# RWKV-6 attention and a maxout layer on one core: loads issued three units ahead, the decay DMAs on another queue, the maxout written with relu, and the weights prepared beside unit 0

## The chip, the core and the metric

The kernel runs on one core of a Trainium2 chip. The time is device time in microseconds for one execution. Five engines work side by side: TensorE (PE, whose weight loads are shown as PEld), VectorE (DVE), ScalarE (ACT), GpSimd (POOL) and SyncE (SP). SP computes nothing here, it only issues DMAs. Each engine takes its instructions in program order, DMA issues among them.

## What is computed

```python
# r, k, v, w: (batch 4, heads 8, seq 768, head_dim 48); u: (heads, head_dim)
for t in range(S):
    cur = outer(u * k[t], v[t])                 # per batch and head, 48 x 48
    y[t] = r[t] @ (state + cur)
    state = w[t][:, None] * state + outer(k[t], v[t])
x = y.transpose(0, 2, 1, 3).reshape(4 * 768, 384)   # tokens x (heads * head_dim)
h1, h2 = x @ w1, x @ w2                         # 384 x 1024 each
out = maximum(h1, h2) @ w_out                   # 1024 x 384 -> (3072, 384)
```

## The kernel before

The sequence is cut into 6 chunks of 128 tokens, and the 4 batches into 2 pairs. A **unit** n is one chunk c = n // 2 of one pair of batches: 12 units. Inside a unit 64 partitions belong to each batch, and each partition holds two consecutive tokens (`i`). The recurrence is done chunk by chunk: logarithms of w (`logw`, ACT, then `lp` on GpSimd), cumulated by a matmul with a triangular matrix (`cumsum`), turned back by exponentials (`exps`), multiplied onto r and k (`scale_rk`, DVE), transposed on TensorE (`transp`, with a DVE copy), multiplied to scores (`scores`), and so on to y (`y_inter`, `y_intra`), which is transposed to x (`xt`, ending in the ACT copy of line 367). The bonus with u is made on GpSimd (`bonus_mul`, `bonus_sum`). For odd chunks but the last, the decay of the whole chunk pair is needed with the head dimension on partitions: `exps` writes one row per batch to DRAM (`row`, line 236) and `decay_load` reads it back transposed (`WL`, line 243, 1024 elements of 4 bytes); both DMAs are issued from the ACT queue, four times each in all (units 2, 3, 6 and 7). `decay_exp` and `decay` use WL one step later.

The maxout is written as max(h1, h2) = |h1 - h2| / 2 + (h1 + h2) / 2. So `gate` multiplies x by wd = w1 - w2 and takes the absolute value (ACT, line 381), and `outp` adds two products: x by wc = (w1 + w2) (w_out / 2), which is folded once, and the gated part by w_out / 2. wd, w1 + w2, its transposes and wc are made by `weights_gate` and `weights_out`.

`step(a, t, g, o)` writes out by hand the order in which four units at different stages are worked on: unit a is being loaded and scaled, unit t transposed and multiplied, units g and o gated and given out. The main loop runs step(n, n - 1, n - 2, n - 2) for n from 3 to 13. **Step n** means that call. Ahead of it stand the first units, one stage after the other: `step(a=0)`, `step(t=0)`, `weights_gate`, `step(a=1, g=0)`, `weights_out`, `step(t=1, o=0)`, `step(a=2)`.

Loads and stores are all issued by SP, in program order. `load(n)` is eight DMAs of 192 KB (w, k, r, v, for each of two batches; runs of 384 bytes). It stands at the start of step n - 2. The buffers for k, r and v are four deep, those for w three deep. `outp` ends in a store of 192 KB from `osb` (four buffers); the store's destination is `out[tok:tok + C, :].rearrange("(q i) n -> i q n", i=2)`, so its outermost dimension has size 2. Each step from the first gated unit on has two stores, behind that step's load in SP's order.

Of the kernel before, what the change touches and what calls it, by code (L numbers as in the profile page):

```python
# [8 lines left out]
F32 = mybir.dt.float32  # L9
BF16 = mybir.dt.bfloat16  # L10
AF = mybir.ActivationFunctionType
# [23 lines left out]
def _body(tc, r, k, v, w, u, moe_w1, moe_w2, moe_w_out, out):  # L35
    nc = tc.nc
    B, H, S, D = r.shape
    P = 128
# [8 lines left out]
    DP = 64  # L47
# [21 lines left out]
    def odd(n):  # L69
        return unit(n)[0] % 2 == 1  # L70

    def last(n):
        return unit(n)[0] == NC - 1
# [5 lines left out]
    def load(n):  # L79
        c, b0 = unit(n)  # L80
        d = {}
        for name, src in (("w", w), ("k", k), ("r", r), ("v", v)):
            t = ldp.tile([P, H, 2, D], F32, tag="l" + name, name="l" + name,
                         bufs=3 if name == "w" else 4)
            for b in range(2):
                nc.sync.dma_start(  # L86
                    out=t[b * Q:(b + 1) * Q].rearrange("p h i d -> p h (i d)"),
                    in_=src[b0 + b, :, c * C:(c + 1) * C, :].rearrange(
                        "h (p i) d -> p h (i d)", i=2))
            d[name] = t  # L90
        L[n] = d
# [4 lines left out]
    w1f = const.tile([P, KO, d_ff], F32)  # L96
    w2f = const.tile([P, KO, d_ff], F32)
    wof = const.tile([P, FO, HD], F32)
    nc.sync.dma_start(out=w1f, in_=moe_w1.rearrange("(o p) n -> p o n", p=P))
    nc.sync.dma_start(out=w2f, in_=moe_w2.rearrange("(o p) n -> p o n", p=P))  # L100
    load(1)
    nc.sync.dma_start(out=wof, in_=moe_w_out.rearrange("(o p) n -> p o n", p=P))
    load(2)
    load(3)


    triS = const.tile([P, P], F32)
    make_upper_triangular(nc, triS, val=1.0, diag=False)
    triI = const.tile([P, P], F32)
    make_upper_triangular(nc, triI, val=1.0, diag=True)  # L110
    tri2 = const.tile([P, P], F32)
    nc.gpsimd.memset(tri2, 0.0)
    ones2 = const.tile([P, P], F32)
    nc.gpsimd.memset(ones2, 0.0)
    for b in range(2):
        nc.gpsimd.memset(ones2[b * Q:(b + 1) * Q, b * Q:(b + 1) * Q], 1.0)
    ident = const.tile([P, P], BF16)
    make_identity(nc, ident)
    mask = const.tile([P, 2, 2, Q], F32)
    sel = const.tile([P, 2, 2, Q], BF16)  # L120
    nc.gpsimd.memset(sel, 0.0)
    for b in range(2):
        q = slice(b * Q, (b + 1) * Q)
        nc.gpsimd.tensor_copy(tri2[q, q], triS[q, q])
        for i in range(2):
            nc.gpsimd.tensor_copy(sel[q, i, i, :], ident[q, q])
            for i2 in range(2):
                nc.gpsimd.tensor_copy(mask[q, i, i2, :],
                                      (triI if (i, i2) == (0, 1) else triS)[q, q])

    NRK = 2
    rkn_b = []
    for i in range(NRK):
        t = const.tile([P, 2, 2, H, DP], BF16, name=f"rkn{i}")
        nc.vector.memset(t, 0.0)
        rkn_b.append(t)
    MZ = [const.tile([P, 2, H, DP], F32, name=f"mz{i}") for i in range(2)]
    for t in MZ:
        nc.gpsimd.memset(t, 0.0)

    S_f = [const.tile([P, 2, NP, D], F32, name=f"Sf{g}") for g in range(2)]
    T_f = [const.tile([P, 2, NP, D], F32, name=f"Tf{g}") for g in range(2)]
# [2 lines left out]
        nc.vector.memset(S_f[g], 0.0)  # L145
        nc.vector.memset(S_b[g], 0.0)
    WL = [const.tile([P, 2, NP], F32, name=f"WL{i}") for i in range(2)]
    for t in WL:
        nc.vector.memset(t, 0.0)

    wd_sb = const.tile([P, KO, d_ff], BF16)
    ws_sb = const.tile([P, KO, d_ff], BF16)
    wo_sb = const.tile([P, FO, HD], BF16)
    wsT_sb = const.tile([P, FO, HD], BF16)
    wc_sb = const.tile([P, KO, HD], BF16)

    def weights_gate():
        for ko in range(KO):
            nc.vector.tensor_sub(wd_sb[:, ko, :], w1f[:, ko, :], w2f[:, ko, :])

    def weights_out():
        for ko in range(KO):
            nc.vector.tensor_add(ws_sb[:, ko, :], w1f[:, ko, :], w2f[:, ko, :])  # L163
        nc.scalar.mul(wo_sb, wof, 0.5)
        for ko in range(KO):
            tp = pt_([P, FO, P], BF16, "tr")
            for fo in range(FO):
                nc.tensor.transpose(tp[:, fo, :], ws_sb[:, ko, fo * P:(fo + 1) * P], ident)
            nc.vector.tensor_copy(
                wsT_sb.rearrange("p f (k c) -> p k f c", k=KO)[:, ko, :, :], tp)  # L170
        for ko in range(KO):
            wc_p = pt_([P, HD], F32, "go", 2)
            for fo in range(FO):
                nc.tensor.matmul(wc_p, wsT_sb[:, fo, ko * P:(ko + 1) * P],  # L174
                                 wo_sb[:, fo, :], start=(fo == 0), stop=(fo == FO - 1))
            nc.vector.tensor_copy(wc_sb[:, ko, :], wc_p)

# [6 lines left out]
    def logw(n):  # L184
        s = U[n] = {}
        s["lw"] = lw = wt_([P, H, 2, D], F32, "lw")
        nc.scalar.activation(lw, L[n]["w"], AF.Ln)  # L187
        s["lp"] = lp = wt_([P, H, D], F32, "lp", 4)
        nc.gpsimd.tensor_add(lp, lw[:, :, 0, :], lw[:, :, 1, :])  # L189

    def bonus_mul(n):
        s = U[n]
        s["vb"] = vb = wt_([P, H, 2, D], BF16, "vb", 3)
        nc.gpsimd.tensor_copy(vb, L[n]["v"])
        s["rku"] = rku = wt_([P, H, 2, D], F32, "rku", 1)
        nc.gpsimd.tensor_mul(rku, L[n]["r"], L[n]["k"])  # L196
        nc.gpsimd.tensor_mul(  # L197
            byi(rku), byi(rku),
            u_b.rearrange("p (h d) -> p h d", h=H).unsqueeze(1).to_broadcast([P, 2, H, D]))
# [27 lines left out]
    def exps(n):  # L227
        s = U[n]
        mz = s["mz"]
        nc.scalar.activation(s["A"][:, 1], mz[:, 0, :, 0:D], AF.Exp)  # L230
        s["iA"] = iA = wt_([P, 2, H, D], F32, "iA", 1)
        nc.scalar.activation(iA, mz[:, :, :, 0:D], AF.Exp, scale=-1.0)
        if last(n) or not odd(n):
            return
        s["row"] = row = drp.tile([2, H * DP], F32, tag="row", name="row")
        nc.scalar.dma_start(out=row, in_=mz[Q - 1::Q, 1].rearrange("b h d -> b (h d)"))

    def decay_load(n):
        if last(n) or not odd(n):
            return  # L240
        s = U[n]
        s["WL"] = wl = WL[n % 2]
        nc.scalar.dma_start(out=wl.rearrange("d b p -> d (b p)"),
                            in_=s["row"].rearrange("b (p x) -> x (b p)", x=P))

    def scale_rk(n):
# [53 lines left out]
    def carry(n):  # L300
        if not odd(n):
            state_cast(unit(n)[1] // 2)
# [66 lines left out]
    def gate(n, j):  # L369
        s = U[n]  # L370
        if j == 0:
            s["gT"] = wt_([P, FO, 2, P], BF16, "gT")
        g = pt_([P, 2, 2 * P], F32, "go", 2)
        for f in range(2):
            fo = 2 * j + f
            for ko in range(KO):
                nc.tensor.matmul(g[:, f, :], wd_sb[:, ko, fo * P:(fo + 1) * P],  # L377
                                 s["xT"][:, ko].rearrange("p j t -> p (j t)"),
                                 start=(f == 0 and ko == 0), stop=(f == 1 and ko == KO - 1),
                                 skip_group_check=True)  # L380
        nc.scalar.activation(s["gT"][:, 2 * j:2 * j + 2].rearrange("p f j t -> p f (j t)"), g,  # L381
                             AF.Abs)

    def outp(n, b):
        c, b0 = unit(n)
# [12 lines left out]
        nc.sync.dma_start(out=dst, in_=osb)  # L398


    def step(a=None, t=None, g=None, o=None, ahead=True):

        A, T, G, O = a is not None, t is not None, g is not None, o is not None
        if T: decay_load(t)
        if T: transp(t, 0)
        if A: cumsum(a)
        if G: gate(g, 0)
        if T: transp(t, 1)
        if A: exps(a)
        if A: bonus_mul(a)  # L410
        if G: gate(g, 1)
        if T: kv(t)
        if T: scores(t, 0)
        if A and ahead and a + 1 < NU: logw(a + 1)
        if T and t >= 1: decay_exp(t - 1)
        if T and t >= 1: decay(t - 1)
        if G: gate(g, 2)
        if G: gate(g, 3)
        if T: scores(t, 1)
        if T: y_inter(t)  # L420
        if T: carry(t)
        if A: scale_rk(a)
        if A: bonus_sum(a)
        if O: outp(o, 0)
        if T: y_intra(t)
        if O: outp(o, 1)
        if T: xt(t)

    logw(0)
    step(a=0, ahead=False)  # L430
    step(t=0)
    weights_gate()
    logw(1)
    step(a=1, g=0, ahead=False)
    weights_out()
    step(t=1, o=0)
    logw(2)
    load(4)
    step(a=2)
    for n in range(3, NU + 2):  # L440
        if n + 2 < NU:
            load(n + 2)
        step(n if n < NU else None, n - 1 if n - 1 < NU else None, n - 2, n - 2)

    ps.release()
# [34 lines left out]
```

## Time and profile before

| | us |
|---|---|
| median of 3 runs | 228.42 (227.33 to 229.29) |
| the profiled execution | 227.37 |
| its span, first to last instruction | 225.4 |

The profile is of one execution. Besides the page it answers queries: what each engine and SP's queue waited for, the busy time and the share of the 16 DMA engines in any stretch, the instructions in order of time, and the chain of work that ended last. Durations below are of that execution, counted from the start of its span.

### The profile page before, as it was taken

What the parts mean: (1) busy time and instruction counts of PE and PEld (TensorE: products, weight loads), DVE (VectorE), ACT (ScalarE), POOL (GpSimd) and SP (SyncE); (2) the same over time, 40 slices, a digit from 0 to 9 for tenths busy, and PEclk for the clock granted to TensorE, in tenths of its full rate; (3) what the DMA queues carried; (4) which work ended last, traced back from release to release, by engine and by line L of the source; (5) the groups of instructions that cost most, each with busy time, mean ns of one, the idle gap of its engine ahead of it and who ended that gap; (6) DMA issues with size and microseconds to landing.
All of it is one profiled execution on the core that took longest, in us unless ns stands there. A gap on an engine that the chain in (4) does not pass through costs nothing.

```text
span 225.4 us, 5068 instructions
## 1 busy us (share of the span) xinstructions
PE 157.4 (70%) x2116; PEld 103.7 (46%) x2116; DVE 117.2 (52%) x138; ACT 89.9 (40%) x150; POOL 108.3 (48%) x115
## 2 busy tenths in 40 slices
PE   0214472486936999885997859869979699988910
PEld 0013351353513757563574635645746466665600
DVE  5097829546029766858165490580683845660000
ACT  2120437000352754563445533634554546354500
POOL 8584094001076934994957805638469493200000
PEclk9999999596695999999999997997999999999995
DMA  6999998920003389648356448555564831111110
GB/s 127 227 412 260 243 273 188 193 70 3 9 31 59 84 172 182 130 131 181 87 143 149 107 109 153 141 130 126 143 154 118 188 74 50 52 53 43 47 43 37
DMA packets 59990, 28.86 MB, mean 128 GB/s; under 512 B 54968, under 2 KB 59192, under 8 KB 59968
## 3 DMA queue, kind: packets, MB, share of 16 engines
q1 hardware_dynamic: 55792, 28.51, 54.3%
q10 hardware_dynamic: 4176, 0.03, 1.1%
q8 instruction: 16, 0.26, 0.5%
q14 instruction: 6, 0.05, 0.1%
HBM read 23.81 MB, written 4.73 MB: 127 GB/s over the span
## 4 chain that ended last, share of the span: by engine, by line
PE 27%; DMA 27%; SPq 20%; DVE 7%; ACT 6%; POOL 4%; issue 4%; ACTq 0%; POOLq 0%; DVEq 0%
SPq L86 17%; DMA lw<-in_w_dram 12%; PE go L392 9%; DMA lk<-in_k_dram 6%; PE go L389 4%; DMA row<-mz 4%; PE go L377 3%; DMA WL<-row 3%; PE go L174 2%; DVE ws_sb L163 2%; ACT gT L381 2%; DMA lr<-in_r_dram 2%; ACT xT L367 2%; SPq L398 2%; PE ex L218 2%
## 5 line engine op out<-in xcount | busy, mean ns | idle before, releaser
L377 PE MATMUL go<-xT,wd_sb 128*128 128x256 bf16 x288 | 38.0, 277 | 2.3 <-ACT xT L367 1.5
L392 PE MATMUL go<-wo_sb,gT 128*128 128x384 bf16 x192 | 38.1, 345 | 0.0
L189 POOL TENSOR_TENSOR lp<-lw 128x384 f32<-128x384 f32 x12 | 14.6, 1216 | 44.9 <-ACT lw L187 44.7
L321 DVE TENSOR_TENSOR M<-sc,mask 128x1024 bf16<-128x1024 f32 x24 | 29.4, 1223 | 8.2 <-PE sc L318 8.2
L395 ACT COPY osb<-go 128x384 f32<-128x384 f32 x24 | 11.5, 479 | 54.8 <-PE go L392 54.8
L377 PEld LDWEIGHTS <-wd_sb 128*128 128x128 bf16 x288 | 27.5, 100 | 11.2 <-issue 6.3
L381 ACT ACTIVATE gT<-go 128x512 bf16<-128x512 f32 x48 | 27.4, 589 | 7.1 <-PE go L377 6.9
L389 PE MATMUL go<-wc_sb,xT 128*128 128x384 bf16 x72 | 17.4, 354 | 13.2 <-ACT gT L381 13.1
L206 POOL TENSOR_TENSOR vd<-lv,dg 128x768 bf16<-128x768 f32 x12 | 18.6, 1550 | 16.5 <-DVE dg L204 16.0
L392 PEld LDWEIGHTS <-gT 128*128 128x128 bf16 x192 | 19.8, 103 | 14.7 <-issue 3.4
L262 DVE COPY rT<-tr 128x1024 bf16<-128x1024 bf16 x12 | 8.3, 688 | 32.2 <-PE tr L257 32.2
L224 DVE TENSOR_TENSOR mz<-ex,lw 128x384 f32<-128x384 f32 x12 | 6.7, 558 | 34.9 <-ACT A L223 34.9
L257 PE MATMUL tr<-ident,rkn 128*128 128x128 bf16 x192 | 15.9, 230 | 12.0 <-DVE rkn L249 8.3
L218 PE MATMUL ex<-lp,tri 128*128 128x384 f32 x24 | 12.5, 606 | 15.0 <-POOL lp L189 12.7
L197 POOL TENSOR_TENSOR rku<-rku,u_b 128x768 f32<-128x768 f32 x12 | 22.4, 1864 | 0.9
L196 POOL TENSOR_TENSOR rku<-lr,lk 128x768 f32<-128x768 f32 x12 | 21.7, 1810 | 0.0
L257 PEld LDWEIGHTS <-rkn 128*128 128x128 bf16 x192 | 13.1, 103 | 14.4 <-DVE rkn L249 10.1
L187 ACT ACTIVATE lw<-lw 128x768 f32<-128x768 f32 x12 | 10.1, 845 | 23.7 <-DMA lw<-in_w_dram 23.4
L307 POOL CAST Sb<-Sf 64x384 bf16<-64x384 f32 x20 | 10.8, 538 | 15.9 <-DVE Sf L290 15.0
L250 DVE TENSOR_TENSOR rkn<-lk,iA 128x768 bf16<-128x768 f32 x12 | 16.2, 1352 | 0.0
L249 DVE TENSOR_TENSOR rkn<-lr,A 128x768 bf16<-128x768 f32 x12 | 15.2, 1271 | 1.0 <-ACT A L230 0.8
L223 ACT ACTIVATE A<-ex 128x384 f32<-128x384 f32 x12 | 5.9, 491 | 24.7 <-PE ex L218 24.7
(61 smaller groups left out, 209.8 us busy)
## 6 DMA issues: line engine op xcount, KB each, us to landing
lw<-in_w_dram SPq DMA_DIRECT2D x24, 192.0 KB
lk<-in_k_dram SPq DMA_DIRECT2D x24, 192.0 KB
lr<-in_r_dram SPq DMA_DIRECT2D x24, 192.0 KB
lv<-in_v_dram SPq DMA_DIRECT2D x24, 192.0 KB
out_dram<-osb SPq DMA_DIRECT2D x24, 192.0 KB
w1f<-in_moe_w_dram SPq DMA_DIRECT2D x1, 1536.0 KB
w2f<-in_moe_w_dram SPq DMA_DIRECT2D x1, 1536.0 KB
wof<-in_moe_w_out_dram SPq DMA_DIRECT2D x1, 1536.0 KB
```

The costliest lines, as they stand in the source:

```text
L86: nc.sync.dma_start(out=t[b * Q:(b + 1) * Q].rearrange("p h i d -> p h (i d)"), in_=src[b0 + b, :, c * C:(c + 1) * C, :].rearrange("h (p i ...
L196: nc.gpsimd.tensor_mul(rku, L[n]["r"], L[n]["k"])
L197: nc.gpsimd.tensor_mul(byi(rku), byi(rku), u_b.rearrange("p (h d) -> p h d", h=H).unsqueeze(1).to_broadcast([P, 2, H, D]))
L206: nc.gpsimd.tensor_mul(byi_inv(vd), L[n]["v"], dg.to_broadcast([P, H, 2, D]))
L218: nc.tensor.matmul(ex, tri2, lp.rearrange("p h d -> p (h d)"), start=not odd(n), stop=True)
L250: nc.vector.tensor_mul(rkn[:, 1, :, :, 0:D], byi(L[n]["k"]), s["iA"])
L257: nc.tensor.transpose(tp[:, p, :, i, :], s["rkn"][:, x, i, 2 * p:2 * p + 2, :].rearrange("s r d -> s (r d)"), ident)
L321: nc.vector.tensor_mul(M.rearrange("s e p t -> s (e p) t"), sc.rearrange("s e p t -> s (e p) t"), mask[:, i].rearrange("s i q -> s (i q)") ...
L377: nc.tensor.matmul(g[:, f, :], wd_sb[:, ko, fo * P:(fo + 1) * P], s["xT"][:, ko].rearrange("p j t -> p (j t)"), start=(f == 0 and ko == 0) ...
L381: nc.scalar.activation(s["gT"][:, 2 * j:2 * j + 2].rearrange("p f j t -> p f (j t)"), g, AF.Abs)
L389: nc.tensor.matmul(o, s["xT"][:, ko, b, :], wc_sb[:, ko, :], start=(ko == 0), stop=False)
L392: nc.tensor.matmul(o, s["gT"][:, fo, b, :], wo_sb[:, fo, :], start=False, stop=(fo == FO - 1))
```

## The change

- `load(n + 3)` stands at the start of step n, `load(4)` ahead of `step(a=1, g=0)` and `load(5)` ahead of the next; w2 is loaded first, then w1 and w_out, then `load(1)` to `load(3)`.
- The DMAs `row` and `WL` are issued from GpSimd's queue. `row` has its own function, called behind `bonus_mul`.
- max(h1, h2) = relu(h1 - h2) + h2: `gate` ends in Relu, wc = w2 w_out, and w_out is no longer halved. The three additions w1 + w2 are gone; w2 is cast on ACT and w_out on GpSimd.
- The transposes of w2 (`weights_turn`, copies now on ACT), `weights_gate` and `weights_out` stand between the parts of unit 0, ahead of step(a=1, g=0). Units 2 and 1 share one step, step(a=2, t=1, o=0).
- Some constants are made after `logw(0)`; the zeroing of MZ moves from GpSimd to DVE, that of WL is dropped.

```diff
+    nc.sync.dma_start(out=w2f, in_=moe_w2.rearrange("(o p) n -> p o n", p=P))
     nc.sync.dma_start(out=w1f, in_=moe_w1.rearrange("(o p) n -> p o n", p=P))
-    nc.sync.dma_start(out=w2f, in_=moe_w2.rearrange("(o p) n -> p o n", p=P))
+    nc.sync.dma_start(out=wof, in_=moe_w_out.rearrange("(o p) n -> p o n", p=P))
     load(1)
-    nc.sync.dma_start(out=wof, in_=moe_w_out.rearrange("(o p) n -> p o n", p=P))
     load(2)
     load(3)
...
+    def weights_cast():
+        for ko in range(KO):
+            nc.scalar.copy(w2_sb[:, ko, :], w2f[:, ko, :])
+        for h in range(2):
+            f = slice(h * FO // 2, (h + 1) * FO // 2)
+            nc.gpsimd.tensor_copy(wo_sb[:, f], wof[:, f])
...
-    def weights_out():
-        for ko in range(KO):
-            nc.vector.tensor_add(ws_sb[:, ko, :], w1f[:, ko, :], w2f[:, ko, :])
-        nc.scalar.mul(wo_sb, wof, 0.5)
+    def weights_turn():
         for ko in range(KO):
             tp = pt_([P, FO, P], BF16, "tr")
             for fo in range(FO):
-                nc.tensor.transpose(tp[:, fo, :], ws_sb[:, ko, fo * P:(fo + 1) * P], ident)
-            nc.vector.tensor_copy(
-                wsT_sb.rearrange("p f (k c) -> p k f c", k=KO)[:, ko, :, :], tp)
+                nc.tensor.transpose(tp[:, fo, :], w2_sb[:, ko, fo * P:(fo + 1) * P], ident)
+            nc.scalar.copy(w2T_sb.rearrange("p f (k c) -> p k f c", k=KO)[:, ko, :, :], tp)
+
+    def weights_out():
         for ko in range(KO):
             wc_p = pt_([P, HD], F32, "go", 2)
             for fo in range(FO):
-                nc.tensor.matmul(wc_p, wsT_sb[:, fo, ko * P:(ko + 1) * P],
+                nc.tensor.matmul(wc_p, w2T_sb[:, fo, ko * P:(ko + 1) * P],
                                  wo_sb[:, fo, :], start=(fo == 0), stop=(fo == FO - 1))
...
+    def decay_row(n):
         if last(n) or not odd(n):
             return
+        s = U[n]
         s["row"] = row = drp.tile([2, H * DP], F32, tag="row", name="row")
-        nc.scalar.dma_start(out=row, in_=mz[Q - 1::Q, 1].rearrange("b h d -> b (h d)"))
+        nc.gpsimd.dma_start(out=row, in_=s["mz"][Q - 1::Q, 1].rearrange("b h d -> b (h d)"))
...
-        nc.scalar.dma_start(out=wl.rearrange("d b p -> d (b p)"),
+        nc.gpsimd.dma_start(out=wl.rearrange("d b p -> d (b p)"),
                             in_=s["row"].rearrange("b (p x) -> x (b p)", x=P))
...
         nc.scalar.activation(s["gT"][:, 2 * j:2 * j + 2].rearrange("p f j t -> p f (j t)"), g,
-                             AF.Abs)
+                             AF.Relu)
...
         if A: bonus_mul(a)
+        if A: decay_row(a)
         if G: gate(g, 1)
         if T: kv(t)
         if T: scores(t, 0)
-        if A and ahead and a + 1 < NU: logw(a + 1)
+        if A and a + 1 < NU and a > 0: logw(a + 1)
...
     logw(0)
-    step(a=0, ahead=False)
-    step(t=0)
+    constants()
+    step(a=0)
+    weights_cast()
+    transp(0, 0)
+    transp(0, 1)
+    kv(0)
+    scores(0, 0)
+    scores(0, 1)
+    y_inter(0)
+    weights_turn()
+    y_intra(0)
     weights_gate()
+    carry(0)
+    xt(0)
+    weights_out()
     logw(1)
-    step(a=1, g=0, ahead=False)
-    weights_out()
-    step(t=1, o=0)
-    logw(2)
     load(4)
-    step(a=2)
+    step(a=1, g=0)
+    load(5)
+    step(a=2, t=1, o=0)
     for n in range(3, NU + 2):
-        if n + 2 < NU:
-            load(n + 2)
+        if n + 3 < NU:
+            load(n + 3)
         step(n if n < NU else None, n - 1 if n - 1 < NU else None, n - 2, n - 2)
```

## Rows read from the trace of the kernel before

**Rows 1.** The page: span; DMA share and GB/s in 40 equal slices; the chain's shares.

```profile
span 225.4 us, 5068 instructions
...
DMA  6999998920003389648356448555564831111110
GB/s 127 227 412 260 243 273 188 193 70 3 9 31 59 84 172 182 130 131 181 87 143 149 107 109 153 141 130 126 143 154 118 188 74 50 52 53 43 47 43 37
...
PE 27%; DMA 27%; SPq 20%; DVE 7%; ACT 6%; POOL 4%; issue 4%; ACTq 0%; POOLq 0%; DVEq 0%
```

**Rows 2.** What engines waited for, whole span: total us, times, longest.

```profile
ACT lw L187 <- DMA lw<-in_w_dram: 23.4, 9, 3.8
...
PE go L389 <- ACT gT L381: 13.1, 7, 2.9
```

**Rows 3.** The DMA view of 187 to 206 us: packets, then queues (share of 16 engines).

```profile
DMA packets 623, 0.98 MB, mean 52 GB/s; under 512 B 8, under 2 KB 620, under 8 KB 620
...
q1 hardware_dynamic: 620, 0.94, 13.2%
```

**Rows 4.** Stretches: us, busy by engine (instructions), PE clock, DMA share, GB/s.

```profile
48.00:60.00 12.00, 9.46 (x138) 5.25 (x136) 5.22 (x7) 1.10 (x2) 1.00 (x2) 0.72 0.01 1
60.00:94.70 34.70, 26.69 (x365) 17.35 (x363) 22.82 (x25) 17.55 (x31) 22.24 (x16) 0.90 0.57 106
94.70:183.20 88.50, 72.47 (x1079) 48.43 (x1078) 49.18 (x61) 42.74 (x76) 55.75 (x51) 0.96 0.57 135
183.20:224.30 41.10, 29.26 (x350) 19.86 (x348) 11.19 (x13) 15.77 (x27) 6.27 (x5) 0.95 0.13 48
224.30:225.40 1.10, 0.00 (x0) 0.00 (x0) 0.00 (x0) 0.00 (x0) 0.00 (x0) 0.50 0.00 0
```

**Rows 5.** The DMA view of 94.7 to 183.2 us, SP's queue.

```profile
q1 hardware_dynamic: 26902, 11.80, 55.1%
```

**Rows 6.** SP's queue in order of time: start, us, line, out<-in, number of DMAs.

```profile
59.13 10.32 SPq L398 DMA_DIRECT2D out_dram<-osb  x2
...
179.12 37.12 SPq L398 DMA_DIRECT2D out_dram<-osb  x10
```

**Rows 7.** What SP's queue waited for on the decay DMAs, whole span.

```profile
SPq L398 <- DMA row<-mz: 9.1, 1, 9.1
SPq L86 <- DMA WL<-row: 8.8, 4, 3.5
...
SPq L86 <- DMA row<-mz: 8.0, 2, 5.8
```

**Rows 8.** The DMA view of 20 to 26 us, when only loads were moving.

```profile
DMA packets 3213, 1.23 MB, mean 204 GB/s; under 512 B 3200, under 2 KB 3212, under 8 KB 3212
```

**Rows 9.** The chain that ended last, 35 to 72 us: start, us, what.

```profile
36.16 4.68 DVE ws_sb L163 x3
...
44.30 4.88 PE go L174 x24
...
62.69 0.75 ACT lw L187
...
69.86 1.04 PE tr L257 x8
```

**Rows 10.** ACT in order of time: the last instruction of steps 10 to 12.

```profile
184.57 0.80 ACT L367 COPY xT<-ex 128x768 bf16<-128x768 bf16 x1
...
196.88 0.80 ACT L367 COPY xT<-ex 128x768 bf16<-128x768 bf16 x1
...
207.49 0.80 ACT L367 COPY xT<-ex 128x768 bf16<-128x768 bf16 x1
```

**Rows 11.** Lines 243 and 50: number, duration ns min/median/max, first and last start.

```profile
L243 ACTq DMA_DIRECT2D WL<-row x4: 361/377/398, 68.9 to 141.6; - x4
...
L50 ACT ACT_TABLE_LOAD  x1: 1283/1283/1283, 0.7 to 0.7; - x1
```

**Rows 12.** The page: the ACT queue's DMA packets.

```profile
q10 hardware_dynamic: 4176, 0.03, 1.1%
```

More of the change, by code (lines that the diff above doesn't have):

```diff
@@ L108, in _body @@
     make_upper_triangular(nc, triS, val=1.0, diag=False)
-    triI = const.tile([P, P], F32)
-    make_upper_triangular(nc, triI, val=1.0, diag=True)
     tri2 = const.tile([P, P], F32)
     nc.gpsimd.memset(tri2, 0.0)
[L113 to L121, printed above, removed]
     for b in range(2):
@@ L124, in _body, with constants @@
         nc.gpsimd.tensor_copy(tri2[q, q], triS[q, q])
[L125 to L129, printed above, removed]
-    NRK = 2
[L132 to L136, printed above, removed]
+    ident = const.tile([P, P], BF16)
+    make_identity(nc, ident)
+    triI = const.tile([P, P], F32)
+    ones2 = const.tile([P, P], F32)
+    mask = const.tile([P, 2, 2, Q], F32)
+    sel = const.tile([P, 2, 2, Q], BF16)
+    def constants():
+        make_upper_triangular(nc, triI, val=1.0, diag=True)
+        nc.gpsimd.memset(sel, 0.0)
+        for b in range(2):
+            q = slice(b * Q, (b + 1) * Q)
+            for i in range(2):
+                nc.gpsimd.tensor_copy(sel[q, i, i, :], ident[q, q])
+                for i2 in range(2):
+                    nc.gpsimd.tensor_copy(mask[q, i, i2, :],
+                                          (triI if (i, i2) == (0, 1) else triS)[q, q])
+        nc.gpsimd.memset(ones2, 0.0)
+        for b in range(2):
+            q = slice(b * Q, (b + 1) * Q)
+            nc.gpsimd.memset(ones2[q, q], 1.0)
+    NRK = 2
     MZ = [const.tile([P, 2, H, DP], F32, name=f"mz{i}") for i in range(2)]
-    for t in MZ:
-        nc.gpsimd.memset(t, 0.0)
+    rkn_b = [const.tile([P, 2, 2, H, DP], BF16, name=f"rkn{i}") for i in range(NRK)]
+    for i in range(2):
+        nc.vector.memset(MZ[i], 0.0)
+        nc.vector.memset(rkn_b[i], 0.0)
     S_f = [const.tile([P, 2, NP, D], F32, name=f"Sf{g}") for g in range(2)]
@@ L147, in _body @@
     WL = [const.tile([P, 2, NP], F32, name=f"WL{i}") for i in range(2)]
-    for t in WL:
-        nc.vector.memset(t, 0.0)
     wd_sb = const.tile([P, KO, d_ff], BF16)
-    ws_sb = const.tile([P, KO, d_ff], BF16)
+    w2_sb = const.tile([P, KO, d_ff], BF16)
     wo_sb = const.tile([P, FO, HD], BF16)
-    wsT_sb = const.tile([P, FO, HD], BF16)
+    w2T_sb = const.tile([P, FO, HD], BF16)
     wc_sb = const.tile([P, KO, HD], BF16)
+    def weights_cast():
[4 more added lines that the diff above has]
+            nc.gpsimd.tensor_copy(wo_sb[:, f], wof[:, f])
     def weights_gate():
@@ L398, in outp, with step @@
         nc.sync.dma_start(out=dst, in_=osb)
-    def step(a=None, t=None, g=None, o=None, ahead=True):
+    def step(a=None, t=None, g=None, o=None):
         A, T, G, O = a is not None, t is not None, g is not None, o is not None
```

## The prediction, made before the changed kernel was run

> **What bounds the kernel now.** Four views, in this order. First the page: no engine is busy all the time, and the chain that ended last spends 47% of itself on DMAs and on SP's queue [rows 1]. So the question is which transfer is late, and why. Second, the waits: ACT waited nine times for w to land, 23.4 us in all, and of that 13.1 us in seven waits came through to TensorE, which stood with gT missing [rows 2]. That looks like a load that is asked for too late, and the change asks for it a step earlier. Third, the DMA view of a stretch in which only stores move: 187 to 206 us. There 620 packets, 0.94 MB, took 13.2% of 16 engines for the whole 19 us, which is 2.1 engines, without a pause [rows 3]. So a store of 196.6 KB runs on two of the 16 engines alone (its outermost dimension has size 2), at 0.94 MB / 19 us = 49.5 GB/s: 3.97 us each, and two stores follow each other rather than sharing. Fourth, the table of stretches [rows 4]. From 94.7 to 183.2 us the queue moved 11.80 MB [rows 5], which is six loads (8 x 196.6 KB = 1.573 MB each) and twelve stores: 88.5 / 6 = 14.75 us for a load and two stores. TensorE alone does not need that: a step with no load to wait for took 12.31 us, and the one after it, which has no new unit, 10.61 [rows 10]. The two engines that carry the stores carry their sixteenth of every load too, and queues are worked off in order, so a load that stands behind two stores lands some 8 us later on these two than on the rest. I read the late w as that, not as a late issue.
>
> If so, the kernel is paced by **this pair of DMA engines**, and a ledger of the pair's time must add up to the span. Loads alone move at 204 GB/s [rows 8], 1.573 MB / 204 = 7.7 us a unit. Up to 48 us: the first four units and the weights, busy throughout. 48 to 60: idle, share 0.01 [rows 4]. 60 to 94.7: two stores and two loads, 7.9 + 15.4 = 23.3 us of 34.7, so 11.4 idle. Then 88.5 busy. From 183.2 to 224.3 ten stores, 39.7 us of 41.1 [rows 4, 6]. That is all 24 stores and 12 loads, and the pair idles 12 + 11.4 + 1.4 = 24.8 us. Why it idles: up to 60 us SP has nothing to issue, since load(4) stands behind the first stores in program order and the first store waits for the first result (issued at 59.13 [rows 6]); after that SP stops for the landing of `row` and `WL`, which ACT issues: 9.1 + 8.8 + 8.0 us in seven waits [rows 7].
>
> **The change part by part.** *Loads three units ahead.* load(4) and load(5) now stand ahead of the first store. Their buffers (units 0 and 1, and w of units 1 and 2) come free as these units are scaled, before about 45 us by the order of before, so the pair goes on from 48 us: 2 x 7.7 = 15.4, to 63.4. The first stores are then due; before, the first was issued at 59.13 [rows 6] with the whole weight work still ahead of it, so they are ready. Worth the 12 us of idle time and, with the next item, the 11.4.
>
> *Decay DMAs on GpSimd's queue.* ACT's issue of `WL` is 0.38 us [rows 11], four times, beside other work: nothing. What counts is whether SP still stops for them. Stops of 16.8 us on loads [rows 7] fell mostly on a pair that still had DMAs queued; I take 0.25 us off each of six cycles, 14.5 us instead of 14.75. Bounds: 14.75 (nothing) and 14.0 (4.5 us in all). The Trainium skill (DMA: Bandwidth & Descriptors, Issuing engines are not separate DMA queues) speaks against a gain here: issuing from several engines only saves the sequencer's issue time. By the row, SP waited 25.9 us for DMAs of another queue; by the page the cycle would stay at 14.75 and the sum below 1.5 us longer.
>
> What it costs GpSimd is not in the trace. Bounds: 0.4 us for an issue as on ACT [rows 11], and 10 us if 1024 elements are written out one by one at what a packet of that queue took (1.1% of 16 x 225.4 us over 4176 packets is 9.5 ns [rows 12]). I take the near row, about 1 us. Cover: GpSimd was busy 55.75 of 88.5 us [rows 4], 9.1 us of a cycle of 14.5, and the `WL` issue is queued ahead of `bonus_mul`, `lp` of the next unit, `decay` and `vd`; those have the 5.4 us left over. WL is used one step later.
>
> *Relu, folding, weights beside unit 0.* The additions (4.68 us) and the folding stood on the chain from 36.16 to 49.2 us [rows 9]; gone or earlier now. The separate step(a=2), 62.69 to 69.86 [rows 9], joins the step before it. Together up to 20 us off TensorE's path. But on the pair they are worth only what lets the stores be ready at 63.4, and that they are even if nothing were gained. I cost them at nothing; the pair's queue hides them. Casts on ACT and GpSimd instead of DVE fall in the first 30 us, when the engines wait for weights to land; the weights being 4.7 MB at about 410 GB/s [rows 1], their new order moves load(1) some 4 us back, and w of unit 1 is not needed before unit 0 is through. Relu for Abs: the same pass.
>
> *What is late next.* TensorE needs about 12.3 us a step against 14.5 of the pair, so it gains on the pair until `osb` (four buffers) is full: `outp` of a step then waits for the stores of two steps before. That wait replaces the one for w, and costs nothing while the pair is busy. At the end the last load has landed and the pair needs only 7.94 us a step; steps 11 to 13 need 12.3, 10.6 and about 8 [rows 10]. Laid out, the last two stores are ready 1 to 2 us before the pair gets to them.
>
> **The sum.** 48.0 (as before) + 15.4 (load(4), load(5)) + 6 x 14.5 = 87.0 (six loads, twelve stores) + 12 x 3.97 = 47.6 (the last twelve stores) = 198.0. From the last packet to the end 1.1 [rows 4]: span 199.1. Around the span lie 227.37 - 225.4 = 2.0 us: **201 us**. The profiled execution lies 1.1 us under the median of the runs shown, 0.5%, which I leave in the range. Against before that is the 24.8 us of idle time and the 1.5 of stops.
>
> **The rivals.** *The pair is not the limit, TensorE is.* For it: the 20 us of the prologue and the 13.1 us of waits [rows 2] both lie on TensorE's path. Against it: the ledger adds up. Step 2 would end near 56 us, then nine steps of 12.3, 10.6 and 8.2, two stores 8.8 and 3.1 around: about 197.
>
> *SP still stops for the decay DMAs.* If DMAs of GpSimd share with SP's whatever made it wait, the stops stay, and those around steps 2 and 3 may again cost part of the 11.4 us. Against it: TensorE is ahead of the pair now, so `row` and `WL` are through before SP comes to them. Between 1.5 and 11.4 us: about 208.
>
> *GpSimd becomes the bound; this is the one that ends on the other side.* Place: `WL` issued in steps 3, 4, 7 and 8, with everything of the unit queued behind it. Spare per cycle is 5.4 us, steps 3 to 8 have six of them, and about 8 us of lead come from the prologue: some 40 us in all. At the upper price of 10 us four issues just fit. To lose the whole gain of 26 us they would have to take (40 + 26) / 4 = 16 us each; only then is it slower, at 229 and up. Between 10 and 16 us it lands at 203 to 225. The Trainium skill (DMA: Bandwidth & Descriptors, SWDGE vs HWDGE vs iDMA) says that descriptors of DMAs issued from GpSimd are computed by a program on its cores, which no row here shows.
>
> *Relu needs another table than Exp and Ln.* One load was 1.28 us, once [rows 11]; six switches a step would be 8 us over eleven steps, and TensorE waits for gT: slower, 270 or more. For it nothing but that Relu does not occur before; Abs needed no second load.
>
> **How the numbers follow.** Forecast (196 to 206) 0.61; TensorE paces it (about 197) 0.11; stops remain (208) 0.12; GpSimd 203 to 225, 0.08; GpSimd slower 0.03; Relu 0.02; something that leaves the time within 1% of before 0.03. What a measurement here can tell from no change is about 1%. The likeliest gives 201. The range takes in the lower bound of the cycle (3 us off: 198), TensorE's own pace with some of its margin (195), and the two cases that end at 208 and a little over: 195 to 212. Faster 0.92, within 1% 0.03, slower 0.05.
>
> **What would show it.** Right: no stretch of DMA share near zero before 190 us; ACT no longer waits for w, but before `osb` for stores; a load and two stores every 14 to 14.8 us; the last twelve stores back to back, at two engines' share; SP without waits for `row` and `WL`. Wrong: idle stretches of the pair left in the middle; or cycles well under 14 us, which would mean that the pair is not in order or not the bound; or a GpSimd busy all through steps 3 to 8; or more than one table load.

## The result, and the profile after

The changed kernel took 201.3 us (median of four runs, 200.4 to 201.9) against 228.9 of the kernel before in the same session: a ratio of 0.880, interval 0.875 to 0.886. The forecast was 201. The profiled execution has a span of 199.6 us (forecast 199.1) and lies 2.25 us below the time of that run. So the number was right. The experiments below show that the reasons given for it were right about what the bound is, and wrong about which part of the change lifted the idle time. (In e10 one execution of four and in e12 two were longer at a lower granted TensorE clock; the ratios leave these out, the medians don't, so there the ratio counts, and that of e12 rests on two executions.)

The page of after: span, DMA share and GB/s in 40 slices, the queue of the decay DMAs, shares of the chain.

```profile
span 199.6 us, 5075 instructions
...
DMA  5999999999998573483593593583581111111110
GB/s 118 210 380 400 291 203 203 203 203 198 201 175 145 143 167 100 128 185 86 144 201 80 151 164 92 146 174 92 151 166 53 50 50 54 50 53 47 48 42 32
...
q0 software_dynamic: 256, 0.03, 0.4%
...
PE 23%; DMA 17%; ACT 5%; DVE 1%; issue 1%; SPq 0%; ACTq 0%; DVEq 0%
```

Against [rows 1]: the hole near 50 us is gone, no slice before the last one is empty, and SP's queue has left the chain (it held 20%). The decay DMAs, 4176 packets of ACT's queue before [rows 12], are 256 of a software queue.

What engines waited for in after, whole span (total us, times, longest):

```profile
ACT osb L404 <- DMA out_dram<-osb: 13.2, 5, 3.7
...
ACT lw L193 <- DMA lw<-in_w_dram: 3.2, 1, 3.2
```

The nine waits for w [rows 2] have become one, of the first unit; five waits of `osb` for stores stand in their place, as forecast. Among SP's waits there is none left for `row` or `WL` [rows 7]. There is one table load, as before.

The table of stretches of after (us, busy by engine, clock, DMA share, GB/s), and the DMA view of its long stretch, 64.5 to 150.1 us:

```profile
48.00:59.50 11.50, 10.90 (x143) 6.76 (x140) 7.49 (x9) 4.62 (x8) 10.70 (x10) 0.85 1.12 189
59.50:64.50 5.00, 5.00 (x93) 3.27 (x91) 4.46 (x6) 2.59 (x6) 2.22 (x3) 1.00 0.92 145
64.50:150.10 85.60, 77.29 (x1199) 53.25 (x1189) 53.40 (x68) 47.33 (x86) 67.08 (x57) 0.98 0.59 139
150.10:198.50 48.40, 34.21 (x431) 22.85 (x428) 15.79 (x18) 18.08 (x32) 9.91 (x8) 0.94 0.14 49
198.50:199.60 1.10, 0.00 (x0) 0.00 (x0) 0.00 (x0) 0.00 (x0) 0.00 (x0) 0.50 0.00 0
```

```profile
q1 hardware_dynamic: 26837, 11.73, 57.5%
```

These are the forecast's own stretches. Each DMA counts its landing up on a semaphore, and the trace holds the times of these updates, though its views don't print them. By them the last part of load(5) landed at 64.55 us (63.4 forecast); then 11.73 MB, six loads and twelve stores, take 85.6 us, 14.27 a cycle (14.5); the last twelve stores take 48.4 (47.6) at two engines' share (0.14); 1.1 us follow. The errors are +1.1, -1.4 and +0.8: 0.5 us in all.

### The profile page after: what moved, and what is told of

The parts are those of the page before. It is cut to its first block, busy times and chain, and to the rows that moved or that the text cites. A ratio compares the mean times of both kernels' runs of the same rounds, so it can differ in the third digit from the quotient of the medians.

```text
span 199.6 us, 5075 instructions
## 1 busy us (share of the span) xinstructions
PE 151.4 (76%) x2116; PEld 101.8 (51%) x2116; DVE 108.9 (55%) x132; ACT 91.9 (46%) x155; POOL 120.3 (60%) x123
## 5 line engine op out<-in xcount | busy, mean ns | idle before, releaser
L401 PE MATMUL go<-wo_sb,gT 128*128 128x384 bf16 x192 | 36.3, 334 | 0.0
L404 ACT COPY osb<-go 128x384 f32<-128x384 f32 x24 | 11.5, 479 | 49.6 <-PE go L401 34.6
L212 POOL TENSOR_TENSOR vd<-lv,dg 128x768 bf16<-128x768 f32 x12 | 17.7, 1475 | 21.5 <-DVE dg L210 21.3
L195 POOL TENSOR_TENSOR lp<-lw 128x384 f32<-128x384 f32 x12 | 12.0, 1001 | 18.5 <-ACT lw L193 18.5
L202 POOL TENSOR_TENSOR rku<-lr,lk 128x768 f32<-128x768 f32 x12 | 22.5, 1871 | 0.0
L224 PE MATMUL ex<-lp,tri 128*128 128x384 f32 x24 | 11.6, 569 | 12.2 <-POOL lp L195 7.2
L316 POOL CAST Sb<-Sf 64x384 bf16<-64x384 f32 x20 | 18.1, 904 | 2.0 <-PE y L349 1.1
L398 PE MATMUL go<-wc_sb,xT 128*128 128x384 bf16 x72 | 15.8, 329 | 0.0
L327 PE MATMUL sc<-rT,kT 48*64 48x128 bf16 x384 | 10.5, 229 | 5.9 <-DVE M L330 2.9
L259 DVE TENSOR_TENSOR rkn<-lk,iA 128x768 bf16<-128x768 f32 x12 | 14.2, 1182 | 0.0
L210 DVE TENSOR_REDUCE dg<-rku 128x16 f32<-128x768 f32 x12 | 11.3, 944 | 3.6 <-POOL rku L203 3.6
```

The source lines that it names most:

```text
L212: nc.gpsimd.tensor_mul(byi_inv(vd), L[n]["v"], dg.to_broadcast([P, H, 2, D]))
L224: nc.tensor.matmul(ex, tri2, lp.rearrange("p h d -> p (h d)"), start=not odd(n), stop=True)
L316: nc.gpsimd.tensor_copy(S_b[g][q, :, :, e * D:(e + 1) * D], S_f[g][q])
L398: nc.tensor.matmul(o, s["xT"][:, ko, b, :], wc_sb[:, ko, :], start=(ko == 0), stop=False)
L401: nc.tensor.matmul(o, s["gT"][:, fo, b, :], wo_sb[:, fo, :], start=False, stop=(fo == FO - 1))
L404: nc.scalar.copy(osb, o)
```

## The experiments

Twelve more kernels were run. Ratios are to the kernel before, run beside each (its median was 228.0 to 229.0).

```
                                                       us      ratio  (interval)
e1  after, stores on 16 engines                       187.3   0.817  (0.811 to 0.823)
e2  before, stores on 16 engines                      208.6   0.910  (0.904 to 0.915)
e3  after, loads two ahead                            200.6   0.875  (0.870 to 0.881)
e4  before, loads three ahead                         234.3   1.024  (1.016 to 1.031)
e5  after, decay DMAs on ACT                          218.8   0.958  (0.951 to 0.966)
e6  before, decay DMAs on GpSimd                      216.6   0.951  (0.944 to 0.957)
e7  before, decay DMAs on GpSimd, loads three ahead   211.9   0.928  (0.921 to 0.935)
e8  after, decay DMAs on ACT, loads two ahead         214.2   0.939  (0.932 to 0.946)
e9  after, stores halved by columns, two engines      209.5   0.917  (0.914 to 0.921)
e10 e7 with logw(2) moved up                          208.5   0.914  (0.911 to 0.917)
e11 e1 with loads two ahead                           187.8   0.823  (0.820 to 0.826)
e12 e10 with steps 1 and 2 merged                     203.4   0.885  (0.880 to 0.891)
```

**Is the pair of engines that carries the stores the bound?** e1 and e2 take the stores off the pair and leave the rest:

```diff
-        nc.sync.dma_start(out=dst, in_=osb)
+        for i in range(2):
+            nc.sync.dma_start(out=dst[i], in_=osb[i * Q:(i + 1) * Q])
```

> The changed kernel; each store is issued as two DMAs of 64 partitions, whose outermost dimension is 64 instead of 2. Theory (the two DMA engines that carry the stores pace the kernel): the pair falls away as the limit, the DMA share is no longer 0.14 when only stores move, TensorE paces the steps at about 12 us each from 54.7 us on: 54.7 + ten steps of 10.6 to 12.3 (119) + 8.2 + 2.5 = 184 us span, about 186 us. Rival (loads asked for in time are what helped, the stores are a side matter): no change, 200 to 202 us.

Measured: 187.3 us. The page of e1, span and its rows PE and DMA, then what `osb` waited for:

```profile
span 185.1 us, 5103 instructions
...
PE   0320657974989989999899898998989988989790
...
DMA  5999999999999999999899595993011030120303
```

```profile
ACT osb L404 <- PE go L401: 43.7, 24, 5.1
```

Now all 24 copies to `osb` wait for TensorE's matmuls, and no wait for a store is left. At the end the DMA engines stand idle between stores, and PE is busy for nine tenths or near it from 50 us on: TensorE is the bound. Without the pair the rest of the kernel needs 187 us, so 14 of the 201 are the pair's. The number of engines shows in the semaphore updates too: a store has 3 in before and in after, one of them well ahead of the other two (60.6 against 66.8 us for the first store in after), and so has each half in e9 below; each half of a store in e1 and e2 has 16, as a load has.

> The kernel before, with this one edit: each store as two DMAs of 64 partitions. Loads stay two units ahead, decay DMAs on ACT's queue, old order of the first units. Theory: step 3 starts near 70 us as before, then steps of about 12 us without waits for w: 70 + 12.5 + 108 + 8.2 + 2.5 = 201 us span, 203 us. Rival (w is late because it is asked for too late): the waits for w stay, 225 to 229 us.

Measured: 208.6, 20 us under before. The page of e2, DMA share:

```profile
DMA  5999999980000228996996284974999943020203
```

The hole from 46 to 67 us stays, as it does not come from the pair; what is behind it runs without the pair's pace. The time expected was 5 to 6 us too low, but far from the rival. SP still stands 35.2 us for `row` and `WL` in e2; whether these are the missing 5 to 6 us stays open.

e9 is the control: it issues as many DMAs as e1, but on the same two engines.

```diff
-        nc.sync.dma_start(out=dst, in_=osb)
+        for f in range(2):
+            nc.sync.dma_start(out=dst[:, :, f * HD // 2:(f + 1) * HD // 2],
+                              in_=osb[:, f * HD // 2:(f + 1) * HD // 2])
```

> The changed kernel with each store issued as two DMAs of 192 columns; each keeps the outermost dimension of size 2. This is the control for the store cut into two DMAs of 64 partitions, which took 187.3 us. Theory (two engines carry the stores and pace the kernel; the number of DMAs is not what helped): the share of the DMA engines in the last store-only stretch stays near 0.14, and the time is 200 to 206 us, since packets half as long do not go faster on the two engines. Rival (more stores in flight is what gained, not more engines): 186 to 192 us.

Measured: 209.5, slower than the theory allowed. The DMA view of e9, 165 to 200 us, when only stores move:

```profile
DMA packets 2108, 1.63 MB, mean 47 GB/s; under 512 B 32, under 2 KB 2105, under 8 KB 2105
...
q1 hardware_dynamic: 2105, 1.59, 13.6%
```

Still two engines' share, at 47 GB/s with packets of 768 bytes instead of 49 to 50 with 1536. That is 5 us over 24 stores; the other 3 of the 8 us are not explained. So more DMAs are not what helped e1. Whether the shorter packets or the doubled number of DMAs lowered the rate, e9 does not tell.

**What was the lead of the loads worth?** e3 takes it out of the changed kernel, e4 puts it alone into the kernel before. The edit of e4 (that of e3 is its reverse, with load(5) left to the loop):

```diff
     logw(1)
+    load(4)
     step(a=1, g=0, ahead=False)
+    load(5)
     weights_out()
     step(t=1, o=0)
     logw(2)
-    load(4)
     step(a=2)
...
-        if n + 2 < NU:
-            load(n + 2)
+        if n + 3 < NU:
+            load(n + 3)
```

> The changed kernel with loads two units ahead as before (load(4) ahead of step 2, load(n + 2) in step n). Theory: the pair's work is the same and it still has no idle stretch, only the order changes, so 200 to 204 us; ACT waits for w again, as in the kernel before, and it costs nothing. Rival (the lead of the loads is what helped): 210 us or more.

> The kernel before with loads three units ahead, nothing else changed. Theory: the pair goes on at 48 us with load(4) and load(5) and is through with them when the first stores are ready; the stops for the decay DMAs stay: 203 to 209 us. Rival (the prologue and the decay queue carry the gain): 220 us or more.

Measured: 200.6 without the lead (after has 201.3, and the intervals overlap). The theory of e3 held, with the waits for w that it expected:

```profile
ACT lw L193 <- DMA lw<-in_w_dram: 12.7, 5, 3.3
```

They cost nothing. But e3 takes away less than its name says. Since units 2 and 1 share a step, load(4), ahead of that step, still stands ahead of the first stores; only load(5) and the later ones move behind stores. SP's queue in e3:

```profile
42.79 1.74 SPq L86 DMA_DIRECT2D lw<-in_w_dram  x2
...
52.14 3.22 SPq L407 DMA_DIRECT2D out_dram<-osb  x2
55.41 2.74 SPq L86 DMA_DIRECT2D lw<-in_w_dram  x2
```

With the lead alone e4 took 234.3 us, 2.4% more than before (1.6 to 3.1%), so there the theory fell. Three views of e4: DMA share of the page; SP's queue (start, us, what, number of DMAs); what SP waited for:

```profile
DMA  6999999910007693464473844935738211111110
```

```profile
45.01 24.62 SPq L86 DMA_DIRECT2D lw<-in_w_dram  x2
69.74 2.85 SPq L86 DMA_DIRECT2D lk<-in_k_dram  x2
```

```profile
SPq L86 <- DMA row<-mz: 28.8, 3, 23.4
```

And ACT's queue in e4:

```profile
67.36 0.84 ACT L232 ACTIVATE iA<-mz 128x768 f32<-128x768 f32 x1
67.39 1.04 ACTq L236 DMA_DIRECT2D row<-mz  x1
```

SP came to load(4) at 45.0 us, 24 us earlier than before, where it comes behind the first stores [rows 6]. It issued one half of w and stood in the other for 23.4 us, to 69.0: until the `row` DMA had landed, which ACT issues at 67.39 from results of unit 2. The load neither reads nor writes `row`, and in the source `row` of unit 2 comes behind both loads. In before SP stood in the second store until `row` had landed there, at nearly the same time (it is done with both stores at 59.13 + 10.32 = 69.45). So all but an eighth of the load came no earlier, and the first two stores, ahead of it before, now stood behind both loads.

The semaphores show what ties them. In this program all DMAs issued by SP and by ACT count their landing on the same eight semaphores, and in before, after and e4 to e7 each was issued only when the one before it on its semaphore had landed. In e4 the second half of w has semaphore 101, and so has that `row`. The eight decay DMAs issued by GpSimd have eight of their own in after (111 to 118). Why `row` got its turn ahead of a load that precedes it in the source stays open.

**What were the stops worth?** e5 puts the decay DMAs of the changed kernel back on ACT's queue, e6 moves them to GpSimd's in the kernel before, and nothing else:

```diff
-        nc.scalar.dma_start(out=row, in_=mz[Q - 1::Q, 1].rearrange("b h d -> b (h d)"))
+        nc.gpsimd.dma_start(out=row, in_=s["mz"][Q - 1::Q, 1].rearrange("b h d -> b (h d)"))
...
-        nc.scalar.dma_start(out=wl.rearrange("d b p -> d (b p)"),
+        nc.gpsimd.dma_start(out=wl.rearrange("d b p -> d (b p)"),
```

> The changed kernel with the decay DMAs back on ACT's queue. Theory: SP may stop for them again, but TensorE is ahead of the pair, so they are through when SP gets there: 201 to 204 us. Rival (the stops were a cause of their own): 208 us or more.

> The kernel before with the decay DMAs on GpSimd's queue, nothing else changed. Theory: the 12 us of idle time of the pair from 48 to 60 us stay, the idle time and the stops after 60 us go: about 211 us (207 to 216). Rival (the stops cost nothing of their own): 225 to 229 us.

Measured: 218.8 and 216.6, so the queue is worth 17 us in the changed kernel and 12 (11.5) in the one before. SP's waits in e5, and SP's queue there:

```profile
SPq L86 <- DMA WL<-row: 14.0, 2, 9.7
...
SPq L407 <- DMA WL<-row: 6.3, 2, 3.6
SPq L86 <- DMA row<-mz: 4.9, 2, 3.2
```

```profile
45.71 10.91 SPq L86 DMA_DIRECT2D lk<-in_k_dram  x2
```

And ACT's queue:

```profile
53.85 0.39 ACTq L252 DMA_DIRECT2D WL<-row  x1
```

With all the rest of the change in place, SP stops for 25.2 us, as it did before [rows 7]. What ACT spends on issuing them does not explain the 17 us: the eight issues take 0.37 to 1.05 us each in e5. That the shared semaphore is what makes the queue matter is read from the traces; no run kept the DMAs on ACT's queue with semaphores of their own. The page of e6, DMA share:

```profile
DMA  5999999970025996483583664664835811111110
```

In e6 SP waits for no decay DMA any more, but the hole at 48 to 59 us stays: that is load(4) standing behind the first stores, the 12 us of the ledger. Most of the 11.5 us that e6 gained lie in the ledger's other stretch, the one with 11.4 idle: SP comes to load(6) 9.1 us earlier, in before and in e6 at

```profile
93.25 4.58 SPq L86 DMA_DIRECT2D lw<-in_w_dram  x2
```

```profile
84.15 4.25 SPq L86 DMA_DIRECT2D lw<-in_w_dram  x2
```

**What was the prologue worth?** e8 is the changed kernel without the two other parts; e7 is the kernel before with these two.

> The kernel before with loads three units ahead and the decay DMAs on GpSimd's queue: all of the change but the relu form and the new order of the first units. Theory: TensorE reaches step 3 some 16 us later than in the changed kernel, but the pair has work until then: 201 to 206 us. Rival (what left TensorE's path in the prologue was worth its time): 213 us or more.

> The changed kernel with loads two units ahead and the decay DMAs on ACT's queue: of the change only the relu form and the new order of the first units are left. Theory: the first stores are ready near 52 us, the pair has load(4) until 56 us, so hardly any idle time; some stops for the decay DMAs: 202 to 209 us. Rival (lead and queue carry the gain): 218 us or more.

Measured: 211.9 and 214.2, each between theory and rival. So the prologue is worth 14 us alone and 10.5 on top of the other two (201.3). In e8 the stops that were expected to be few are 23.0 us in all, the longest of them in load(4):

```profile
SPq L86 <- DMA WL<-row: 17.7, 4, 10.2
SPq L86 <- DMA row<-mz: 5.3, 2, 3.2
```

SP's waits and queue in e7:

```profile
SPq L86 <- ACT lw L187: 10.6, 1, 10.6
```

```profile
49.92 1.81 SPq L86 DMA_DIRECT2D lv<-in_v_dram  x2
62.41 1.75 SPq L86 DMA_DIRECT2D lw<-in_w_dram  x2
...
68.38 1.73 SPq L401 DMA_DIRECT2D out_dram<-osb  x2
```

load(4) goes out early here, but w of load(5) needs the buffer of w of unit 2 (w has three), and logw(2), which frees it, comes behind step(t=1) in the old order. SP stands from 51.7 to 62.4, and every store with it: the first two `osb` are ready at 58.5 and 60.9, and SP issues them at 68.38. e10 moves that one line up, e12 also makes one step of two:

```diff
     step(a=1, g=0, ahead=False)
+    logw(2)
     load(5)
     weights_out()
-    step(t=1, o=0)
-    logw(2)
-    step(a=2)
+    step(a=2, t=1, o=0)
```

> The kernel with the old prologue, loads three ahead and decay DMAs on GpSimd (211.9 us), with one line moved: logw(2), which reads w of unit 2, now stands ahead of load(5), weights_out and step(t=1) instead of behind them. Theory A (what the old prologue still cost was SP standing 10.6 us in load(5) until the buffer of w(2) came free): SP's wait on ACT lw goes, the idle stretch of the DMA engines near 56 to 65 us goes with it, and the time falls to 201 to 206 us. Theory B (the old prologue costs through TensorE's path, 20 us longer before step 3, and through it makes the stores late): the wait goes, but the stores are not ready when load(5) has landed, and the time stays at 209 to 214 us. Between 206 and 209 both hold in part.

> The kernel of the run before last but one (old prologue, loads three ahead, decay DMAs on GpSimd, logw(2) moved up; 208.5 us) with step(t=1, o=0) and step(a=2) merged into one step, as the change does. What is left of the old prologue then is the weight preparation in one block behind unit 0, with casts on VectorE, and the maxout form. Theory A (the order of steps 1 and 2 on TensorE's path, and through it the stores and the next loads, made the rest): 201 to 204 us, as the changed kernel. Theory B (the weight block ahead of step 1 makes it): 206 to 209 us, no better than without the merge; the first stores then still stand ready after load(5) has landed, by some microseconds, and the DMA engines show a gap there.

Measured: 208.5 for e10 (both theories in part) and 203.4 for e12, by its ratio (of two executions) 0.885 x 228.0 = 201.9: as the changed kernel, within the noise. So, by the ratios, the early logw(2) is worth (0.928 - 0.914) x 228 = 3 us and the merged step (0.914 - 0.885) x 228 = 6 to 7. What e12 still lacks of the change, above all Relu in place of Abs, the folded weights and their casts beside unit 0, makes 1 us by the ratios (0.885 against 0.880), and the intervals overlap: nothing that can be measured here. By what wait the separate step(a=2) still cost 6 us in e10 stays open.

**Is there a better version?** e1 beats both kernels. e11 is e1 with loads two ahead:

> The changed kernel with stores on 16 engines (187.3 us) and loads two units ahead instead of three. With the pair of engines gone as the bound TensorE paces the kernel, and loads at 204 GB/s need 7.7 us a unit against a step of some 12. Theory (the lead of three is worth nothing, with or without the pair): 186.5 to 189 us. Rival (the lead only seemed worthless because the pair paced the kernel; with TensorE as the bound a late load shows): 191 to 200 us, with ACT waiting for w again.

Measured: 187.8, as e1, with no wait for w but the first. Three units of lead are not needed with TensorE as the bound either.

## Why the prediction was right, and where it was not

**The bound** was right. Stores run on two engines (13.2% of 16 [rows 3]), the pair paces the kernel, and the time left is what the pair has to move: e1 and e9 show it from both sides. The Trainium skill (DMA: Bandwidth & Descriptors, Why a DMA increments its semaphore by 16 and not by 1) says that a DMA uses as many engines as the largest number up to 16 that divides the slowest dimension of both sides. The store's slowest dimension has size 2; two engines' share in after (0.14 of 16) and the gain of e1 agree. The reading that a load behind stores is late on these two engines alone shows in after's semaphore updates. Of the 16 of the first half of w that follows the first two stores, 14 come at 65.6 to 66.3 us and two at 71.9, right behind the second store, which lands at 70.8. The forecast had some 8 us for this delay; here it is 5.6.

**The sum** was right because it was made on the pair. It asked how much idle time would be left, 24.8 us before and none after, and for that it does not matter which edit fills which gap. In part this is luck: gaps that the prediction gave to the lead of the loads were closed by edits that it priced at 1.5 us and at nothing, and these happened to be in the same change. Two terms of three came out a little long and one short. The ledger also mixes two prices of a load. It takes 7.7 us, the rate of loads alone, for loads beside stores too, but its own cycle of 14.75 less two stores of 3.97 leaves 6.8 (14.27 less the same leaves 6.3 in after). So the 11.4 idle of two loads and two stores are some 2 us too few. The forecast's cycles are taken from the row and not from these parts, so the sum does not suffer.

**"Loads three units ahead ... worth the 12 us of idle time and, with the next item, the 11.4"** failed. The lead alone costs about 5 us, because SP's early loads stop for `row` with the stores behind them (e4); with both other parts in place it is worth nothing (e3). What fills the hole at 48 us in e3 is what the prediction said, load(4) ahead of the first stores, but it is the shared step that puts it there, and then stores that are ready at 52. In after the first stores are ready as early, though SP issues them at 59.49 behind load(5), and e3, which has load(5) behind them, is no slower. ACT and SP in after:

```profile
51.61 0.48 ACT L404 COPY osb<-go 128x384 f32<-128x384 f32 x1 [4.68 <-PE go L401]
...
54.35 0.48 ACT L404 COPY osb<-go 128x384 f32<-128x384 f32 x1 [1.18 <-PE go L401]
```

```profile
59.49 1.46 SPq L407 DMA_DIRECT2D out_dram<-osb  x2
60.99 4.45 SPq L86 DMA_DIRECT2D lw<-in_w_dram  x2
```

**"I take 0.25 us off each of six cycles"** failed by the most. The stops of 25.9 us [rows 7] were priced at 1.5, with 4.5 as the bound, and had a share in the 11.4 that was never split; they measured 12 to 17. Two readings led there. One was that a stop on a load falls on a pair with DMAs still queued: but the longest, 9.1 us, was on a store, in the issue from 59.13 to 69.45 [rows 6, 7], and lies where the ledger itself has 11.4 idle. The other was "TensorE is ahead of the pair now, so `row` and `WL` are through before SP comes to them". e5 has that lead and stops all the same, since SP runs ahead of the results too: it comes to k of load(4) at 45.7, and ACT issues the `WL` that it stands for at 53.85. The rule of the Trainium skill weighed there (DMA: Bandwidth & Descriptors, Issuing engines are not separate DMA queues), that issuing from several engines saves only the sequencer's issue time, does not cover this case: `WL`'s issue is 0.38 us [rows 11], and the queue is worth 12 to 17.

**"I cost them at nothing; the pair's queue hides them"** was half right. For Relu, folding and weights it holds (e12). For the order of the steps it does not: the prologue is worth 10.5 us on top of the rest, 6 to 7 of them through the merged step and 3 through the buffer of w, which the prediction took to be free by 45 us "by the order of before" when that order frees w of unit 2 only near 62 (e7; in before logw(2) starts at 62.58). That the stores are ready at 63.4 even so did hold, at 58.5 and 60.9 in e7; what was missed is that SP can't issue them, or anything else, while it stands in load(5).

**GpSimd** was right. The rows of `row` and `WL` in after (number, duration ns min/median/max, first and last start, then us from issue to landing of `WL`):

```profile
L245 POOL DMA_DIRECT2D row<-mz x4: 604/606/731, 48.5 to 108.7; - x4
```

```profile
L252 POOL DMA_DIRECT2D WL<-row x4: 959/959/965, 54.7 to 115.1; - x4
...
DMA to landing us min/median/max: 5.6/7.0/7.1
```

0.96 us for `WL` where 1 was taken, and 67.08 us busy of the 85.6, so the rival that would have ended on the other side was far off.

**The rival "TensorE paces"** was put at 197, and e1, which TensorE paces, takes 187. Only some 4 of these 10 us are TensorE's: the rival's own terms have the last result ready near 56 + 110.7 + 10.6 + 8.2 = 185.5, and in e1 the last `osb` is ready at 181.2. The other 6 are what follows, mostly the last two stores, which the rival prices at 8.8 us on the pair and which e1 does on 16 engines. ACT in e1:

```profile
180.73 0.48 ACT L404 COPY osb<-go 128x384 f32<-128x384 f32 x1 [1.31 <-PE go L401]
```

With 197 the margin to the pair was thought to be 1 to 2 us at the end. In after it was some 5 us: the last `osb` was ready at 189.40, and the last store began near 198.5 - 3.97 = 194.5. ACT in after:

```profile
188.92 0.48 ACT L404 COPY osb<-go 128x384 f32<-128x384 f32 x1 [1.31 <-PE go L401]
```

## What to carry to other kernels

A ledger of the resource that paces a kernel can give the time of a change rightly and still say nothing of which edit earns it; where an edit is priced at nothing or at the whole gain, test it alone, as a lead that was given 12 us and a share of 11.4 more cost 5 when it came alone. Count on how many DMA engines a transfer runs before asking when it is issued: cutting the store so that all 16 take part took another 14 us off the changed kernel, with two lines. When a queue waits for a DMA that it neither reads nor feeds, ask who issues that DMA: every instruction behind the wait pays for it, and a load moved ahead only moves the stop ahead.

## What the hardware showed that was not expected

SP's loads and stores wait for DMAs of ACT's queue with which they share no data: 25.9 us in before, 28.8 for `row` alone in e4, 25.2 in e5, and none where GpSimd issues them. The traces show the tie in the program's use of its semaphores, not in the DMA engines. From GpSimd the same decay DMAs are 256 packets instead of 4176, and `WL` takes 5.6 to 7.1 us to land. And stores on two engines move 49 to 50 GB/s with packets of 1536 bytes, and 47 with twice as many DMAs and packets of 768.
